# Attention and two gated MLPs on one core: another warm-up, another cut of the first MLP, and a planner's numbers anew

## The chip, the core and the metric

The kernel runs on one core of a Trainium2 chip. Time is the device time of one execution in microseconds (us). A core has five engines with queues of their own: TensorE (PE in the profile; its weight loads are PEld), VectorE (DVE), ScalarE (ACT), GpSimd (POOL) and SyncE (SP), which here issues all the transfers. They run side by side and wait for each other by semaphores only.

## The reference

Three stages follow each other; each takes the output of the one before as a matrix of 2304 tokens by 512.

```python
# attention: 4 images, 8 heads, 576 positions, 64 wide
rel = pos[:, None] - pos[None, :]
mask_plain = (rel >= 0) & (rel < 32)                      # heads 0 to 3
mask_dil = (rel >= 0) & (rel < 128) & (rel % 4 == 0)      # heads 4 to 7
attn = softmax(where(mask, q @ k.T / 8, -1e9));  x = attn @ v
# first gated MLP: d_model 512, d_ff 1536
xn = x / sqrt(mean(x * x) + 1e-6) * rms_g
x = (silu(xn @ w_gate) * (xn @ w_val)) @ w_out
# second gated MLP, with other weights of the same sizes
out = (sigmoid(x @ w2_gate) * (x @ w2_val)) @ w2_out
```

All in float32, except that the weights come as 64-bit numbers: the kernel reads both 32-bit words of each and makes a float32 of them.

## The kernel before, in words

**Products in two halves.** TensorE multiplies in a rounded format (fp32r). Each operand is split into a high part (a rounded copy, "hi") and a low part (the rest, "lo"), and each product is three matmuls: hi by hi, hi by lo, lo by hi. The helper `split` (lines 572 to 579) makes hi on ScalarE or VectorE and lo on GpSimd or VectorE.

**Attention.** Two heads are taken together, so there are four pairs for each of four images: pairs 0 and 1 with the plain mask, 2 and 3 with the dilated one. A pair is done in three groups of 192 positions, 48 groups in all. A group is twelve score matmuls (line 932), the mask and row maximum on VectorE (944), the exponential on ScalarE (950), the division, three transposes on TensorE (977), a copy (982), and twelve matmuls with the values (990). The first image's keys and queries are loaded by `first_qk` in long rows and turned on TensorE (784); those of the others are loaded in short rows and turned on VectorE (905). When all groups that a chunk of tokens needs are done, `x_norm` normalises it (sums at 1053, spreading at 1109, scaling at 1121) and splits it.

**First MLP.** The 1536 columns of d_ff are 12 blocks of 128. `PARAMS["holds"]` says in how many parts they are worked through and how many blocks each part keeps in the buffers: (4, 4, 4). In a part, all the chunks of tokens pass; their widths are `PARAMS["sizes"]`: four of 288 tokens and three of 384. For a chunk and a block, `mlp_step` makes the gate and value products (line 1278, twelve matmuls each) and their combination, and `y_group` the output product (line 1320, four times three matmuls). A part after the first loads the normalised chunk and the partial sums again and adds to them (line 1348). The first part runs while the attention is still going on. The weight buffers are two rings: 26 tiles of gate and value weights (four to a block) and 6 of output weights (one to a block).

**Weights.** `words` loads 512 KB into one of three buffers, and converts with one ScalarE (line 553) and four VectorE instructions (556, 559, 562, 565). Weights of the first part are split at once (`weight_plain`); all others are converted early, stored, and loaded again when due (`weight_ahead`, `weight_late`).

**Second MLP.** Three parts of four blocks; the products are formed with seven block products instead of eight (`unit`, line 1540; `y_products`, line 1458), for one image after the other.

**What sets the order.** No queue is written by hand. Each operation is added with an engine (or a choice of engines with a penalty each), an estimated cost, and a due time; `Line.emit` then plays the program through with these costs and, for each engine, takes the operation that can start first, and among those that can start at the same time the one with the earliest due time. The order found is the order of the queues, and is fixed in the program. The transfers are operations of SP, with an estimated rate. The numbers in `PARAMS` set due times (`att0`, `span0`, `lo1`, `hi1` and so on for the groups of each chunk; `wdue`, `wslope` for the weights; `ld_a` to `ld_d` for the first loads), penalties (`w_lo`, `ts`, ...) and earliest starts (`rel1`, `rel2`). Where an order is said in words ("wst order"), operations start in the order of the program.

**Warm-up and fillers.** `warm_up` writes zeros (line 805) and multiplies them (line 812): `warm_n` matmuls in threes, and later `warm_c` runs of `warm_m`, each of which may start from a time on and is left out if it could not start until another. `filler` (line 741) multiplies zeros into a bank that is about to be used, as many times as fit into the wait that the planner sees; `fill_from` and `fill_share` set from which wait on and how many.

Of the kernel before, what the change touches and what calls it, by code (L numbers as in the profile page):

```python
# [8 lines left out]
F32 = mybir.dt.float32  # L9
# [12 lines left out]


PARAMS = {
    "late": 0, "fill_share": -1.645, "fill_max": 6, "gather": -3.359, "w0_hi": 0.17,
    "w0_lo": 1.905, "h0_hi": 0.438, "h0_lo": 1.239, "x0_hi": 1.34, "x0_lo": 11.623, "ahead": 2,
    "todo0": 56.796, "todo1": 25.362, "todo2": 159.576, "todo3": 11.023, "xb_zero": 1.288,
    "stay": 0.699, "phase": 1.6, "fill_from": -2.118, "fill_gap": 0.077, "margin": 2922.227,
    "wait": 1.059, "w_sq": 42.802, "w_hi": 0.161, "w_lo": 1.285, "x_hi": 1.845, "x_lo": 0.0,
    "h_hi": 1.711, "h_lo": 0.003, "qk": 1.905, "norm": 0.0, "pts": 18.659, "o": 0.0, "snap": 7.898,  # L30
    "h_ahead": 98.614, "h2_ahead": -0.542, "evac": 0.038, "holds": (4, 4, 4), "norm_act": 0.0,
    "slack": 0.0, "share_v": 0.6, "share_p": 0.33, "cold": 1.7, "low": 0, "high": 0, "recip": 0.3,
    "rel1": 9.513, "span1": 1.059, "rel2": -0.748, "span2": -34.805, "ys": 37.984, "ts": 4.608,
    "cross": 0.06, "same": 0.04, "dma_lat": 1.7, "dma_rate": 330000.0, "by_pe": 0,
# [3 lines left out]
    "ld_v": -216.171, "ld_c": -161.215, "ld_d": -125.254, "lead": -1.421, "xdue": 1.319,  # L38
    "wdue": 0.824, "wslope": 1.126, "wload": -1350.235, "wload_step": -0.494, "warm_n": 12,
    "warm_t": 1.362, "warm_dt": -2.155, "warm_c": 19, "warm_m": 5, "warm_late": 13.822,  # L40
    "warm_due": 37.022, "mask_cost": 0.18, "exp_cost": 0.36, "s_cost": 0.546, "o_cost": 0.41,
    "t_cost": 0.265, "pt_lead": 1.847, "x_lead": 29.885, "wy_due": 1.584, "y_from": 5.448,
    "y_step": 0.787, "xb_due": -0.013, "y_last": 1.205, "xb_last": 0.798, "lo6": 114.943,
    "hi6": 132.108, "sizes": (288, 288, 288, 288, 384, 384, 384),
}
STEP = 6.24

# [32 lines left out]
class Line:  # L80
# [11 lines left out]

    def __init__(self):
        self.ops, self.writer, self.readers = [], {}, {}
        self.now = self.bus = 0.0
        self.last, self.mate, self.longer = {}, {}, 0.0
        self.work, self.window, self.warm, self.quad = 0.0, 0, False, False

# [43 lines left out]
    def add(self, eng, cost, fn, reads=(), writes=(), tiles=(), due=0.0, lat=0.0,  # L142
            release=0.0, until=None, other=(), bus=0.0, cols=0, fill=None, quad=False):

        o = Op()
        o.ways = {eng: (cost, fn, 0.0)}
        for kind, eng, cost, fn in [other] if other and isinstance(other[0], str) else other:  # L150
            o.ways[eng] = cost, fn, PARAMS[kind]
        o.eng, o.tiles, o.due, o.lat = None, list(tiles), due, lat
        o.seq, o.succs, o.end, o.release = len(self.ops), [], None, release
        o.until, o.bus = until, bus
        o.cols, o.fill, o.fills, o.quad = cols, fill, 0, quad
        preds = set()
        for key in reads:
            if key not in self.writer:
                raise KeyError(key)
            preds.add(self.writer[key])  # L160
            self.readers.setdefault(key, []).append(o)
        ahead = set()
# [18 lines left out]
        self.ops.append(o)  # L181
        return o
# [152 lines left out]
def attention_then_two_gated_mlps(  # L335
# [15 lines left out]
    nc = tc.nc  # L351
# [3 lines left out]
    P = 128  # L355
# [7 lines left out]
    T = S // 2  # L363
# [53 lines left out]
    add = line.add  # L417
    rings = {}

    def new(pool, tag, shape, dt=F32, bufs=2):  # L420
        ring = rings.setdefault((pool, tag), Ring(
            bufs, None if pool in ("mid", "bp") else 0.0, tag))
        return Tile(ring, lambda: pools[pool].tile(shape, dt, tag=tag, name=tag, bufs=bufs), shape)
# [37 lines left out]

    def rows(n, size):

        return n * (16.0 + 0.033 * size) / 16e3 * PARAMS["dma_rate"]


    ident = fixed("sb", "ident", [P, P])
# [288 lines left out]
    def first_qk(b, hp, staging, due, turn_due, engines=("SP", "SP")):  # L756


        dil = hp >= HP // 2
        hk = (b, hp)  # L760
        TP = S // 8
        kt, qt = qk_tiles(hk, turn_due)
        raws = []
        for nm, src, (ring, bufs), eng in zip("kq", (k, q), staging, engines):
            raw = new("sb", ring, [TP, 8, 2, D], F32, bufs)

            def load(raw=raw, src=src):
                (nc.scalar if eng == "ACT" else nc.sync).dma_start(
                    out=raw.t, in_=src[b, 2 * hp:2 * hp + 2].rearrange(
                        "e (p n) d -> p n e d", n=8))  # L770

            dma(load, rows(2 * S, 4 * D), writes=[("raw", nm, hk)] + ["o order"] * (ring == "wo"),
                tiles=[raw], due=due, cost=0.6, eng=eng)
            raws.append(raw)
        for nm, t, off, raw in (("k", kt, 32, raws[0]), ("q", qt, 0, raws[1])):
            for a in range(2):
                turned[0] += 1
                bank = new("ps", ("g", "y3", "v")[turned[0] % 3] if dil else ("g", "y3")[a],
                           [P, 4, TP], F32, 1)

                def turn(raw=raw, a=a, bank=bank):
                    for r in range(4):

                        nc.tensor.transpose(
                            bank.t[:, r], raw.t[:, 4 * a + r].rearrange("p e d -> p (e d)"),
                            ident[0:TP, 0:TP])

                add("PE", 0.255, turn, reads=[("raw", nm, hk), "ident"], writes=[("tb", nm, hk, a)],
                    tiles=[raw, bank], due=turn_due, cols=4 * TP, fill=filler(bank))

                def put(copy, t=t, off=off, a=a, bank=bank):
                    tt = t.t[:, off:off + S]
                    dst = tt.rearrange("p (r q a) -> p a r q" if dil else "p (q a r) -> p a r q",
                                       r=4, a=2)[:, a]
                    copy(out=dst, in_=bank.t)

                add("ACT", 0.36, lambda put=put: put(nc.scalar.copy),
                    reads=[("tb", nm, hk, a), ("kpad", hk)],
                    writes=[(nm + "T", hk, a)], tiles=[bank, t], due=turn_due,
                    other=("qk", "DVE", 0.36, lambda put=put: put(nc.vector.tensor_copy)))  # L800
        heads[hk] = kt, qt

    def warm_up(n, times):

        add("PL", 0.3, lambda: nc.gpsimd.memset(zeros.bitcast(F32), 0.0), writes=["warm"], due=-90)

        def some(n, cost, due, release, until=None):
            bank = new("ps", "y3", [P, T], F32, 1)

            def run():  # L810
                for _ in range(n):
                    nc.tensor.matmul(out=bank.t, lhsT=zeros[:, 0:P], rhs=zeros, start=True, stop=True)

            add("PE", cost, run, reads=["warm"], tiles=[bank], due=due, release=release,
                until=until, cols=n * T)

        for _ in range(n // 3):
            some(3, 0.128 * 3, -90, 0.0)
        for t in times:
            some(PARAMS["warm_m"], 0.128 * PARAMS["warm_m"], PARAMS["warm_due"], t,  # L820
                 t + PARAMS["warm_late"])

    def first_v(due):

# [978 lines left out]
```

## Time and profile before

| | us |
|---|---|
| median of 3 timed runs | 1041.44 (1040.22 to 1044.84) |
| the profiled execution's own time | 1038.41 |
| its span, from the first to the last instruction | 1036.3 |

| engine | busy us | share of the span | instructions |
|---|---|---|---|
| PE | 988.2 | 95% | 7624 |
| PEld | 957.7 | 92% | 7624 |
| DVE | 737.5 | 71% | 1757 |
| ACT | 499.6 | 48% | 1393 |
| POOL | 401.3 | 39% | 572 |

Busy time is the time in which at least one instruction of the engine runs; a matmul counts from its start to its end, and as matmuls overlap, time from one start to the next is shorter than the duration. The shares are means over stretches with different limits. The granted TensorE clock was 0.995 of full speed over the span.

### The profile page before, as it was taken

What the parts mean: (1) busy time and instruction counts of PE and PEld (TensorE: products, weight loads), DVE (VectorE), ACT (ScalarE), POOL (GpSimd) and SP (SyncE); (2) the same over time, 40 slices, a digit from 0 to 9 for tenths busy, and PEclk for the clock granted to TensorE, in tenths of its full rate; (3) what the DMA queues carried; (4) which work ended last, traced back from release to release, by engine and by line L of the source; (5) the groups of instructions that cost most, each with busy time, mean ns of one, the idle gap of its engine ahead of it and who ended that gap; (6) DMA issues with size and microseconds to landing.
All of it is one profiled execution on the core that took longest, in us unless ns stands there. A gap on an engine that the chain in (4) does not pass through costs nothing.

```text
span 1036.3 us, 21382 instructions
## 1 busy us (share of the span) xinstructions
PE 988.2 (95%) x7624; PEld 957.7 (92%) x7624; DVE 737.5 (71%) x1757; ACT 499.6 (48%) x1393; POOL 401.3 (39%) x572
## 2 busy tenths in 40 slices
PE   7889999999999999999999999999999999999997
PEld 6778888989999999999999989998889999999996
DVE  4898877688777778852444586778785769786765
ACT  4978577764542333422222354566563355434432
POOL 3355553466841001340011562346571256533220
PEclk9999999999999999999999999999999999999999
DMA  8859877859899889865776752635163553267633
GB/s 197 174 130 192 211 176 182 213 176 342 319 348 316 324 308 329 303 231 205 247 267 222 245 177 110 229 150 189 58 241 141 193 226 133 99 203 234 167 74 80
DMA packets 207690, 216.62 MB, mean 209 GB/s; under 512 B 136609, under 2 KB 163809, under 8 KB 207585
## 3 DMA queue, kind: packets, MB, share of 16 engines
q1 hardware_dynamic: 207584, 215.27, 65.2%
q8 instruction: 60, 0.98, 0.4%
q14 instruction: 46, 0.37, 0.1%
HBM read 145.23 MB, written 69.99 MB: 208 GB/s over the span
## 4 chain that ended last, share of the span: by engine, by line
PE 73%; DVE 14%; ACT 5%; DMA 3%; issue 2%; POOL 2%; SPq 1%; DVEq 0%; POOLq 0%; ACTq 0%
PE y L1320 13%; PE v L1278 13%; PE g L1278 13%; PE y L1458 11%; PE att L1540 8%; PE v L1540 6%; PE g L1540 5%; DVE t L1157 2%; ACT pr L950 2%; DVE t L1556 2%; PE att L932 1%; DVE h L579 1%; PE att L990 1%; DVE S L652 1%; DVE t L1578 1%
## 5 line engine op out<-in xcount | busy, mean ns | idle before, releaser
L576 POOL TENSOR_TENSOR h<-t,h 128x288 fp32r<-128x288 f32 (+1 forms) x164 | 149.6, 918 | 413.4 <-ACT h L572 365.6
L572 ACT CAST h<-t 128x288 fp32r<-128x288 f32 (+1 forms) x251 | 110.5, 444 | 175.1 <-DVE t L1301 89.7
L1320 PE MATMUL y<-h,wo 128*128 128x288 f32 (+1 forms) x1008 | 169.6, 315 | 0.3 <-ACT pt L1340 0.2
L1278 PE MATMUL v<-xo,w 128*128 128x288 f32 (+1 forms) x1008 | 166.7, 313 | 0.0
L1278 PE MATMUL g<-xo,w 128*128 128x288 f32 (+1 forms) x1008 | 166.7, 313 | 0.0
L1458 PE MATMUL y<-h,wo 128*128 128x288 f32 x1008 | 158.9, 298 | 5.8 <-ACT h L572 1.9
L1320 PEld LDWEIGHTS y<-h,wo 128*128 128x128 f32 x1008 | 154.6, 188 | 1.8 <-ACT pt L1340 0.4
L1278 PEld LDWEIGHTS g<-xo,w 128*128 128x128 f32 x1008 | 155.2, 189 | 0.3 <-issue 0.2
L1278 PEld LDWEIGHTS v<-xo,w 128*128 128x128 f32 x1008 | 154.4, 188 | 0.7
L1458 PEld LDWEIGHTS y<-h,wo 128*128 128x128 f32 x1008 | 142.5, 190 | 8.9 <-ACT h L572 3.0
L1301 DVE TENSOR_TENSOR t<-t,v 128x288 f32<-128x288 f32 (+1 forms) x84 | 41.4, 493 | 80.5 <-PE v L1278 76.3
L1411 DVE SCALAR_TENSOR_TENSOR pt<-y,pt 128x288 f32<-128x288 f32 x136 | 61.2, 452 | 50.1 <-PE y L1458 49.6
L1292 ACT ACTIVATE t<-g 128x288 f32<-128x288 f32 (+1 forms) x56 | 25.0, 447 | 94.8 <-PE g L1278 94.8
L1556 DVE TENSOR_TENSOR t<-t,att 128x288 f32<-128x288 f32 x96 | 43.0, 447 | 30.2 <-PE att L1540 26.0
L579 DVE TENSOR_TENSOR h<-t,h 128x288 fp32r<-128x288 f32 (+1 forms) x88 | 49.8, 571 | 14.3 <-ACT h L572 12.2
L950 ACT ACTIVATE pr<-pr,nmx 128x96 f32<-128x96 f32 x144 | 52.2, 365 | 11.6 <-DVE nmx L944 11.5
L562 DVE SCALAR_TENSOR_TENSOR wz<-wst,wz 128x512 int32<-128x512 int32 x72 | 55.8, 778 | 1.4
L565 DVE SCALAR_TENSOR_TENSOR wz<-wst,wz 128x512 int32<-128x512 int32 x72 | 55.6, 773 | 1.1
L553 ACT ACTIVATE wz<-wst 128x512 f32<-128x512 f32 x72 | 47.5, 668 | 17.6 <-DMA wst<-in_moe_w_gate_dram 7.8
L1540 PE MATMUL att<-xo,w 128*128 128x288 f32 x336 | 53.9, 295 | 1.0 <-DVE t L1556 1.0
L1540 PE MATMUL att<-wst,w 128*128 128x288 f32 x336 | 54.1, 296 | 0.0
L1157 DVE TENSOR_TENSOR t<-t,t 128x288 f32<-128x288 f32 x82 | 52.6, 642 | 1.3 <-POOL h L576 0.7
(193 smaller groups left out, 1764.4 us busy)
## 6 DMA issues: line engine op xcount, KB each, us to landing
z<-wz SPq DMA_DIRECT2D x60, 256.0 KB, 4.4
xo<-xs SPq DMA_DIRECT2D x23, 576.0 KB, 6.4
wst<-in_moe_w_gate_dram SPq DMA_DIRECT2D x24, 512.0 KB, 5.9
wst<-in_moe_w_val_dram SPq DMA_DIRECT2D x24, 512.0 KB, 5.4
wst<-in_moe_w_out_dram SPq DMA_DIRECT2D x24, 512.0 KB, 5.2
xs<-xs SPq DMA_DIRECT2D x21, 576.0 KB, 5.8
wst<-xs SPq DMA_DIRECT2D x18, 576.0 KB, 6.7
xo<-x SPq DMA_DIRECT2D x16, 576.0 KB, 5.5
```

Of the source, the lines that this page charges most:

```text
L562: add("DVE", Shared(0.595), lambda: nc.vector.scalar_tensor_tensor(out=z.t, in0=top(), scalar=-0x40000000, in1=z.t, op0=ALU.bitwise_and, o ...
L572: add("ACT", act(n), lambda: nc.scalar.copy(out=hi(), in_=src()), reads=reads, writes=[key] + [order] * bool(order), tiles=tiles + [dst], ...
L576: add("PL", pool(n), lambda: nc.gpsimd.tensor_tensor(out=lo(), in0=src(), in1=hi().bitcast(F32), op=ALU.subtract), reads=reads, writes=[ke ...
L579: other=(kind + "_lo", "DVE", dves(n), lambda: nc.vector.tensor_tensor(out=lo(), in0=src(), in1=hi().bitcast(F32), op=ALU.subtract)))
L950: add("ACT", PARAMS["exp_cost"], lambda u=u: nc.scalar.activation(out=pr.t[:, u], in_=pr.t[:, u], func=ACTF.Exp, bias=nmx.t[:, u:u + 1], s ...
L1157: add("DVE", dves(n), lambda: nc.vector.tensor_tensor(out=dst(), in0=a(), in1=c(), op=ALU.subtract), reads=reads, writes=writes, tiles=til ...
L1278: nc.tensor.matmul(out=bank.t, lhsT=w[:, l, cols], rhs=x[:, r, j], start=kk == 0 and n == 0, stop=kk == KD - 1 and n == 2)
L1320: nc.tensor.matmul(out=yb.t, lhsT=w.t[:, l, s], rhs=h.t[:, r], start=n == 0 and j == 0, stop=n == HOLDS[p] - 1 and j == 2)
L1411: add("DVE", dve(T), lambda: nc.vector.scalar_tensor_tensor(out=t.t[:, e, h], in0=bank.t, scalar=0.5, in1=t.t[:, e, h], op0=ALU.mult, op1= ...
L1458: nc.tensor.matmul(out=bank.t, lhsT=w.t[:, u, a, n], rhs=hs[u].t[:, d], start=first and u == 0 and m == 0, stop=u == NF // 2 - 1 and m == ...
L1540: nc.tensor.matmul(out=bank.t, lhsT=l.t[:, a, cols], rhs=r.t[:, d, j], start=first and j == 0 and m == 0, stop=j == 1 and m == 2, skip_gro ...
L1556: add("DVE", dve(T), lambda: nc.vector.tensor_tensor(out=t.t, in0=t.t, in1=bank.t, op=ALU.add), reads=[(key, uk)], writes=[ck[name]], tile ...
```

## The change

The new zeros' write is due first of all. The warm-up is one operation of 36 matmuls, in one bank that the later runs share. In the planner, the transfers begin at 1.6 us, rows cost 17.5 + 0.0355 per byte in place of 16.0 + 0.033, and a first load of keys or queries takes 1.1 us of SP in place of 0.6. The first MLP is cut into six chunks of 384 tokens and two parts of six blocks. Nearly all numbers in `PARAMS` are others; those that the prediction speaks of stand here, with some more.

```diff
-    "late": 0, "fill_share": -1.645, "fill_max": 6, "gather": -3.359, "w0_hi": 0.17,
+    "late": 0, "fill_share": -0.727, "fill_max": 6, "gather": 0.48, "w0_hi": 18.322,
...
-    "stay": 0.699, "phase": 1.6, "fill_from": -2.118, "fill_gap": 0.077, "margin": 2922.227,
+    "stay": 0.079, "phase": 1.6, "fill_from": 18.077, "fill_gap": -1.297, "margin": 2367.916,
...
-    "h_ahead": 98.614, "h2_ahead": -0.542, "evac": 0.038, "holds": (4, 4, 4), "norm_act": 0.0,
+    "h_ahead": 6.245, "h2_ahead": 1.536, "evac": 4.911, "holds": (6, 6), "norm_act": 0.904,
...
-    "turn0": -125.532, "turn1": -118.934, "turn2": -32.107, "att0": -371.487, "span0": 277.415,
-    "lo1": -10.504, "hi1": 2.607, "lo2": -1.115, "hi2": 13.348, "lo3": 1.504, "hi3": 89.26,
-    "lo4": 41.946, "hi4": 67.51, "lo5": 57.885, "hi5": 113.642, "ld_a": -294.837, "ld_b": -450.833,
-    "ld_v": -216.171, "ld_c": -161.215, "ld_d": -125.254, "lead": -1.421, "xdue": 1.319,
-    "wdue": 0.824, "wslope": 1.126, "wload": -1350.235, "wload_step": -0.494, "warm_n": 12,
-    "warm_t": 1.362, "warm_dt": -2.155, "warm_c": 19, "warm_m": 5, "warm_late": 13.822,
+    "turn0": 4.444, "turn1": -321.528, "turn2": -13.602, "att0": -191.799, "span0": 189.778,
+    "lo1": 2.246, "hi1": 21.361, "lo2": 1.646, "hi2": 44.88, "lo3": 40.955, "hi3": 63.261,
+    "lo4": 76.278, "hi4": 113.005, "lo5": 138.438, "hi5": 87.307, "ld_a": -107.09,
+    "ld_b": -123.163, "ld_v": -63.575, "ld_c": -63.972, "ld_d": -16.401, "lead": 1.069,
+    "xdue": 12.604, "wdue": -1.765, "wslope": 2.786, "wload": -675.096, "wload_step": 8.573,
+    "warm_n": 36, "warm_t": 1.316, "warm_dt": 0.302, "warm_c": 19, "warm_m": 5, "warm_late": 2.625,
...
-    "hi6": 132.108, "sizes": (288, 288, 288, 288, 384, 384, 384),
+    "hi6": 56.455, "sizes": (384, 384, 384, 384, 384, 384),
...
-        self.now = self.bus = 0.0
+        self.now, self.bus = 0.0, 1.6
...
-        return n * (16.0 + 0.033 * size) / 16e3 * PARAMS["dma_rate"]
+        return n * (17.5 + 0.0355 * size) / 16e3 * PARAMS["dma_rate"]
...
-                tiles=[raw], due=due, cost=0.6, eng=eng)
+                tiles=[raw], due=due, cost=1.1, eng=eng)
...
-        add("PL", 0.3, lambda: nc.gpsimd.memset(zeros.bitcast(F32), 0.0), writes=["warm"], due=-90)
-
-        def some(n, cost, due, release, until=None):
-            bank = new("ps", "y3", [P, T], F32, 1)
+        add("PL", 0.3, lambda: nc.gpsimd.memset(zeros.bitcast(F32), 0.0), writes=["warm"], due=-600)
+
+        bank = new("ps", "y3", [P, T], F32, 1)
+
+        def some(n, due, release, until=None):
...
-            add("PE", cost, run, reads=["warm"], tiles=[bank], due=due, release=release,
+            add("PE", 0.128 * n, run, reads=["warm"], tiles=[bank], due=due, release=release,
                 until=until, cols=n * T)
 
-        for _ in range(n // 3):
-            some(3, 0.128 * 3, -90, 0.0)
+        some(n, -90, 0.0)
         for t in times:
-            some(PARAMS["warm_m"], 0.128 * PARAMS["warm_m"], PARAMS["warm_due"], t,
-                 t + PARAMS["warm_late"])
+            some(PARAMS["warm_m"], PARAMS["warm_due"], t, t + PARAMS["warm_late"])
```

## Rows read from the trace of the kernel before

**Rows 1.** Stretches: length, busy us of each engine (instructions), clock, DMA share, GB/s.

```profile
31.00:46.00 15.00, 11.89 (x185) 10.25 (x185) 11.72 (x49) 14.84 (x49) 5.61 (x9) 1.00 1.03 206
46.00:73.40 27.40, 24.21 (x282) 20.98 (x279) 24.76 (x110) 20.98 (x83) 13.09 (x32) 0.94 0.40 91
73.40:118.00 44.60, 40.42 (x431) 37.14 (x430) 36.50 (x121) 32.98 (x117) 23.97 (x43) 1.00 0.88 192
118.00:235.00 117.00, 112.02 (x1170) 104.12 (x1169) 93.77 (x347) 82.38 (x297) 59.85 (x118) 1.00 0.76 196
235.00:594.30 359.30, 358.25 (x2333) 357.95 (x2333) 227.39 (x411) 122.17 (x254) 104.49 (x120) 1.00 0.81 286
594.30:780.00 185.70, 172.79 (x1243) 167.24 (x1242) 142.65 (x255) 104.81 (x270) 97.22 (x107) 0.99 0.46 168
780.00:1036.30 256.30, 244.76 (x1796) 240.16 (x1794) 184.10 (x395) 105.56 (x271) 85.01 (x102) 0.99 0.48 153
```

**Rows 2.** The same view for line 932 alone, the score matmuls.

```profile
0.00:73.40 73.40, 12.03 (x216) 9.81 (x216) 0.98 0.73 161
73.40:118.00 44.60, 5.27 (x96) 4.22 (x96) 1.00 0.88 192
```

**Rows 3.** Chain of waits in order of time: start, us, what.

```profile
249.22 2.08 PE y L1320 x12
...
302.00 1.60 PE y L1320 x12
```

**Rows 4.** Groups by line, shape: count | busy us, mean ns | idle before.

```profile
L1278 PE MATMUL g<-xo,w 128*128 128x288 f32 x576 | 85.7, 297 | 0.0
...
L1278 PE MATMUL g<-xo,w 128*128 128x384 f32 x432 | 81.0, 335 | 0.0
```

**Rows 5.** The same view, VectorE: weight conversion and additions of partial sums.

```profile
L562 DVE SCALAR_TENSOR_TENSOR wz<-wst,wz 128x512 int32<-128x512 int32 x72 | 55.8, 778 | 1.4
L565 DVE SCALAR_TENSOR_TENSOR wz<-wst,wz 128x512 int32<-128x512 int32 x72 | 55.6, 773 | 1.1
...
L559 DVE TENSOR_SCALAR wz<-wz 128x512 int32<-128x512 int32 x72 | 37.5, 527 | 1.2
...
L556 DVE TENSOR_SCALAR wz<-wz 128x512 f32<-128x512 f32 x72 | 35.7, 500 | 21.9 <-ACT wz L553 21.0
...
L1348 DVE SCALAR_TENSOR_TENSOR pt<-y,pt 128x288 f32<-128x288 f32 x32 | 12.8, 451 | 0.0
...
L1348 DVE SCALAR_TENSOR_TENSOR pt<-y,pt 128x384 f32<-128x384 f32 x24 | 12.3, 553 | 0.8 <-PE y L1320 0.8
```

**Rows 6.** Stretches for line 565 alone, the last instruction of a conversion.

```profile
0.00:73.40 73.40, 4.99 (x7) 0.98 0.73 161
73.40:118.00 44.60, 4.62 (x6) 1.00 0.88 192
118.00:140.00 22.00, 2.69 (x4) 1.00 0.84 212
```

**Rows 7.** Timeline, first 45 us: start, us, engine, what, idle before it.

```profile
6.05 9.41 PE L812 MATMUL y<-zeros 128*128 128x288 f32 x27 [6.05 <-POOL zeros L805]
...
15.50 0.68 PE L784 MATMUL v<-ident,xo 72*128 72x72 f32 x4
```

**Rows 8.** Stretches up to 118 us for line 741 alone, the fillers: their sum.

```profile
sum 118.00, PE 16.60 PEld 13.83; mean PE 3.32 PEld 2.77
```

**Rows 9.** Timeline of TensorE from 40 to 75 us.

```profile
41.69 0.45 PE L784 MATMUL g<-ident,wo 72*128 72x72 f32 x4
...
56.37 4.19 PE L741 MATMUL y<-zeros 128*128 128x288 f32 x30
...
63.57 1.06 PE L1278 MATMUL g<-xo,w 128*128 128x288 f32 x6
...
71.12 1.81 PE L1278 MATMUL g<-xo,w 128*128 128x288 f32 x6
```

**Rows 10.** Waits of TensorE from 594.3 us on: total us, times, longest.

```profile
PE g L1540 <- DVE t L1556: 9.2, 8, 2.2
```

More of the change, by code (lines that the diff above doesn't have):

```diff
@@ L24 @@
 PARAMS = {
-    "late": 0, "fill_share": -1.645, "fill_max": 6, "gather": -3.359, "w0_hi": 0.17,
-    "w0_lo": 1.905, "h0_hi": 0.438, "h0_lo": 1.239, "x0_hi": 1.34, "x0_lo": 11.623, "ahead": 2,
-    "todo0": 56.796, "todo1": 25.362, "todo2": 159.576, "todo3": 11.023, "xb_zero": 1.288,
-    "stay": 0.699, "phase": 1.6, "fill_from": -2.118, "fill_gap": 0.077, "margin": 2922.227,
-    "wait": 1.059, "w_sq": 42.802, "w_hi": 0.161, "w_lo": 1.285, "x_hi": 1.845, "x_lo": 0.0,
-    "h_hi": 1.711, "h_lo": 0.003, "qk": 1.905, "norm": 0.0, "pts": 18.659, "o": 0.0, "snap": 7.898,
@@ L31 @@
-    "h_ahead": 98.614, "h2_ahead": -0.542, "evac": 0.038, "holds": (4, 4, 4), "norm_act": 0.0,
-    "slack": 0.0, "share_v": 0.6, "share_p": 0.33, "cold": 1.7, "low": 0, "high": 0, "recip": 0.3,
-    "rel1": 9.513, "span1": 1.059, "rel2": -0.748, "span2": -34.805, "ys": 37.984, "ts": 4.608,
-    "cross": 0.06, "same": 0.04, "dma_lat": 1.7, "dma_rate": 330000.0, "by_pe": 0,
[3 rows of a table removed]
-    "ld_v": -216.171, "ld_c": -161.215, "ld_d": -125.254, "lead": -1.421, "xdue": 1.319,
-    "wdue": 0.824, "wslope": 1.126, "wload": -1350.235, "wload_step": -0.494, "warm_n": 12,
@@ L40 @@
-    "warm_t": 1.362, "warm_dt": -2.155, "warm_c": 19, "warm_m": 5, "warm_late": 13.822,
-    "warm_due": 37.022, "mask_cost": 0.18, "exp_cost": 0.36, "s_cost": 0.546, "o_cost": 0.41,
-    "t_cost": 0.265, "pt_lead": 1.847, "x_lead": 29.885, "wy_due": 1.584, "y_from": 5.448,
-    "y_step": 0.787, "xb_due": -0.013, "y_last": 1.205, "xb_last": 0.798, "lo6": 114.943,
-    "hi6": 132.108, "sizes": (288, 288, 288, 288, 384, 384, 384),
+    "late": 0, "fill_share": -0.727, "fill_max": 6, "gather": 0.48, "w0_hi": 18.322,
@@ new lines @@
+    "w0_lo": 9.893, "h0_hi": 0.962, "h0_lo": 0.547, "x0_hi": 1.123, "x0_lo": 0.752, "ahead": 2,
+    "todo0": 1353.619, "todo1": 6.063, "todo2": 24.639, "todo3": 0.613, "xb_zero": 0.211,
+    "stay": 0.079, "phase": 1.6, "fill_from": 18.077, "fill_gap": -1.297, "margin": 2367.916,
+    "wait": 0.585, "w_sq": 11.505, "w_hi": 0.053, "w_lo": 2.389, "x_hi": 0.018, "x_lo": 0.021,
+    "h_hi": 9.803, "h_lo": 0.002, "qk": 6.776, "norm": 0.38, "pts": 8.075, "o": 0.0, "snap": 2.373,
+    "h_ahead": 6.245, "h2_ahead": 1.536, "evac": 4.911, "holds": (6, 6), "norm_act": 0.904,
@@ new lines @@
+    "slack": 0.0, "share_v": 0.6, "share_p": 0.33, "cold": 1.7, "low": 0, "high": 0.39,
+    "recip": 0.3, "rel1": 84.815, "span1": -1.884, "rel2": 10.263, "span2": 0.38, "ys": 0.0,
+    "ts": 0.246, "cross": 0.06, "same": 0.04, "dma_lat": 1.7, "dma_rate": 330000.0, "by_pe": 0,
[3 rows of a table added]
+    "ld_b": -123.163, "ld_v": -63.575, "ld_c": -63.972, "ld_d": -16.401, "lead": 1.069,
+    "xdue": 12.604, "wdue": -1.765, "wslope": 2.786, "wload": -675.096, "wload_step": 8.573,
+    "warm_n": 36, "warm_t": 1.316, "warm_dt": 0.302, "warm_c": 19, "warm_m": 5, "warm_late": 2.625,
@@ L45 @@
+    "warm_due": 7.242, "mask_cost": 0.18, "exp_cost": 0.36, "s_cost": 0.546, "o_cost": 0.41,
+    "t_cost": 0.265, "pt_lead": 8.857, "x_lead": 16.276, "wy_due": 0.304, "y_from": 5.373,
+    "y_step": 0.87, "xb_due": -0.264, "y_last": 1.124, "xb_last": 9.329, "lo6": 108.574,
+    "hi6": 56.455, "sizes": (384, 384, 384, 384, 384, 384),
 }
```

## The prediction

> **What bounds the kernel now.** I read the stretches first: the busy time of each engine in windows cut where the work changes [rows 1]. They show four regimes. Up to 73.4 us the attention of the first 18 groups runs (216 score matmuls, 12 to a group [rows 2]); ScalarE is full in the middle of it (14.84 of 15.00 us) and TensorE waits or multiplies zeros. From 73.4 to 235 us the first MLP's first part runs between the other 30 groups: TensorE is idle for 44.60 - 40.42 = 4.2 us up to 118 and for 117.00 - 112.02 = 5.0 us after. From 235 to 594.3 us nothing but MLP matmuls is left, and TensorE is busy for 358.25 of 359.30 us: here only TensorE's own time counts. The second MLP follows with 12.9 and 11.5 us of idle TensorE, the last few of them the end of the program. So TensorE is the bound from 73.4 us on; in the first 118 us VectorE and ScalarE press on it.
>
> Then I read what a matmul costs. The chain of waits has twelve of 384 columns in 2.08 us and twelve of 288 in 1.60 us [rows 3], end to end, so 173.3 and 133.3 ns. (The mean duration in the lines view is longer, as matmuls overlap; I take from it the counts alone: 576 and 432 in one of the three products [rows 4].)
>
> **The change, part by part.** Terms are in us against the profiled execution: span 1036.3, its time 1038.4, so 2.1 lie around the span. The timed median, 1041.4, is 3.0 above that execution; I add 3.0 at the end.
>
> *Six chunks of 384.* Three products x 576 = 1728 matmuls of 288 columns become 3 x 432 = 1296 of 384: 1728 x 133.3 ns = 230.4 against 1296 x 173.3 ns = 224.6. **-5.8**, all on the engine that is the bound [rows 3, 4].
>
> Here a rule speaks against the change. The Trainium skill (TensorE: Matmul & The Clock Gate, the formula for the isolated gap) puts a full-clock matmul at columns divided by 2.4 GHz plus 2.5 ns: 122.5 and 162.5 ns, and the term would be 211.7 - 210.6 = -1.1. The chain disagrees: 13.3 ns beyond the columns at either width [rows 3]. I go by the chain.
>
> *Two parts of six blocks instead of three of four.* One reload of partial sums goes: 56 additions at line 1348 (32 + 24) become 24, some 25.6 - 13.3 = 12 us of VectorE [rows 5], with one store and one load of all partial sums and one load of all inputs. They lay where TensorE was idle 1.05 us in 359 [rows 1]: 0. A chunk passes six blocks in the first part instead of four, half as much MLP again, so the remaining attention has more to lie beside. MLP1 took 230.4 + 224.6 = 455.0, 2 before 73.4; of the 520.9 us from there to 594.3, 453 are MLP, 10.2 idle, and 57.7 are 30 groups, 1.9 a group. Those 57.7 stay. Of the idle 9.2 before 235 I take half away, **-4.6** (at best -9.2).
>
> *What is due sooner.* The first chunk now needs 18 converted weights, not 12. A conversion is four VectorE instructions, 500 + 527 + 778 + 773 ns = 2.58 us [rows 5], so six are 15.5. In the trace 7 were done by 73.4 and 6 more by 118, while VectorE worked 36.5 of 44.6 us [rows 1, 6]. But that stretch also finished 8 groups (96 / 12 [rows 2]); the new second chunk needs the two left of the first image and eight of the second, 20 in all, and 18 are there at 73.4. Six groups can move out, and the first chunk's matmuls are as long as the two first chunks of now (6 x 6.24 = 37.4, against 8 x 4.8 = 38.4). I take 0; from below 0, from above the whole 15.5. The six loads, 512 KB each, also go into a stretch where the DMA engines are 0.88 busy.
>
> *Buffers at the seams.* The ring of 26 weight buffers now holds 24 for one part (16 before), the ring of 6 output weights all 6. A split of the next part's weights waits for the last chunk's matmuls of the same block; behind it on ScalarE and GpSimd stand the running block's own casts, for which TensorE waits. Each block frees its buffers one step, 6.24 us, after the one before, five steps ahead of use, so I take **+1** (0 to one step, 6.2).
>
> *The start.* The zeros are written first instead of after the masks (TensorE waited 6.05 us for them [rows 7]); the masks come later by that one write, and no score needs them before the first keys have landed. The 27 warm-up matmuls become one run of 36; the later ones, which may start only within their time limit, mostly fall out. All that lies before the first transposes of keys at 15.5 [rows 7]: 0. The fillers, 16.6 us of zero matmuls [rows 8], go; they filled waits, so nothing is saved. The clock is a cost: granted 0.94 from 46 to 73.4 [rows 1], half speed (1.2 of 2.4 GHz) in one piece at the end of it, where six matmuls took 1.81 us against 1.06 earlier [rows 9]. Without the run of 30 fillers at 56.4 I count such pieces twice or three times: **+1.7** (0 to 5).
>
> That fits a rule, which alone gives no more: the Trainium skill (TensorE: Matmul & The Clock Gate, What's actually happening) has the clock throttled unless recent activity released it. By it the piece filled by the 30 zero matmuls would be slow and the sum the same.
>
> The first chunk is 384 wide: some ten steps in its chain grow by about 0.1 us (451 to 553 ns for one VectorE operation [rows 5]): **+1**. The order of loads and operations follows a planner whose small-row loads cost 9% more and whose issues on SP take 1.1 us, not 0.6; weights still come first, the first plain heads' keys and queries (two issues) now pass ahead of the 13 loads of values. The last head pair's keys reached TensorE at 41.7, and the first MLP matmul came 22 us later [rows 9]: a better order of ScalarE's queue is worth something there, **-3** (-10 to +7, the time between matmuls at 63.6 and 71.1 being 7.5).
>
> *The second MLP.* Only due times and preferences between engines move; there are 24.4 us of idle to win from [rows 1]. One late VectorE product alone costs 9.2 [rows 10]. I take **-1** (-12.9 to +12.9, the first stretch's idle once gone, once doubled).
>
> Sum: -5.8 - 4.6 + 1 + 1.7 + 1 - 3 - 1 = -10.7. The profiled execution would be 1027.7, the median 1031.
>
> **Rivals.** *Weights late in the first chunk (slower).* Conversions keep the present pace: 7 + 6 + 4 = 17 by 140 us [rows 6], the 18th at 142. TensorE would come to block six after 31.2 us of matmuls and some seven groups, 73.4 + 31.2 + 13 = 118: 24 late, of which four more groups (8) can fill. 16 are lost, 1047, and with the half of the idle not won (4.6) 1052. It decides the sign once more than 10 of these 24 us stay unfilled. For it: VectorE and DMA near full. Against: 5 of the conversions counted up to 140 were for later parts.
>
> *Given back (same).* The 5.8 is real, but seams, clock and second MLP stand at the upper ends of the small terms (5 + 3 over mine), or the idle stays: about 1039. For it: every re-ordered stretch has new waits. Against: nothing was idle at the present seams [rows 1].
>
> *A shorter start (faster still).* The order gains its 10, the 9.2 goes wholly, some of the second MLP's idle too: 1017. For it: 63 us before the first MLP matmul, 16.6 of zeros. Against: ScalarE full from 31 to 46.
>
> **How the numbers follow.** 0.5% is 5.2 us, about what a measurement of this kernel tells from no change: faster is below 1036.2, slower above 1046.6. Forecast 0.50 (1022 to 1040; 0.42 of it faster, 0.08 same); late weights 0.16 (slower 0.14, same 0.02); given back 0.16 (same 0.13, slower 0.03); shorter start 0.18 (faster). Faster 0.60, same 0.23, slower 0.17. The range leaves about 0.1 out at either end: 1012 to 1047.
>
> **What would show it.** Right: 2592 matmuls of 384 columns in lines 1278 and 1320, twelve in 2.08; the last of the first MLP near 584 instead of 594.3; no idle TensorE at the one seam between parts near 350 to 360. Start: the first full MLP product before 73.4. Wrong: TensorE waiting for w or wz between 75 and 125; idle in steps of 6 us at a seam; more half-clock pieces before 75 than three; a second MLP longer than 442 us.

## The result, and the profile after the change

The changed kernel took 1025.14 us in the median (1024.38 to 1027.10, 4 runs) against 1040.83 (4 runs) beside it on the same chip: a ratio of 0.9847 [0.9815, 0.9879], 15.7 us less. The forecast was 1031 (10.4 below the 1041.4 that it started from) and its range 1012 to 1047. The profiled execution took 1024.38 with a span of 1022.6, against 1038.4 and 1036.3: 13.7 less in the span. The last matmul of the first MLP ends at 585.05 instead of 594.34 (-9.3), and what follows takes 437.6 instead of 442.0 (-4.4).

First the stretches of the changed kernel, as in [rows 1]: length, busy time (instructions) of TensorE, its weight load, VectorE, ScalarE and GpSimd, granted clock, DMA share, GB/s. The cut at 594.3 became 582, 3 us before the first MLP ends, and that at 780 became 768.

```profile
15.00:31.00 16.00, 14.19 (x160) 11.98 (x158) 11.06 (x62) 14.43 (x55) 9.08 (x20) 0.71 1.02 219
31.00:46.00 15.00, 14.63 (x155) 12.15 (x152) 10.42 (x53) 12.47 (x50) 7.63 (x15) 0.54 0.94 210
46.00:73.40 27.40, 24.87 (x245) 21.32 (x245) 22.97 (x95) 21.88 (x81) 17.21 (x37) 0.81 0.49 114
73.40:118.00 44.60, 39.97 (x377) 34.83 (x375) 39.81 (x113) 30.01 (x102) 29.66 (x51) 0.96 0.91 190
118.00:235.00 117.00, 114.72 (x984) 106.16 (x985) 93.95 (x294) 72.50 (x246) 62.98 (x120) 0.99 0.76 196
235.00:582.00 347.00, 346.73 (x2077) 344.20 (x2076) 215.61 (x397) 119.82 (x245) 108.27 (x128) 1.00 0.67 228
582.00:768.00 186.00, 174.95 (x1260) 168.61 (x1259) 147.86 (x266) 97.30 (x259) 106.05 (x116) 1.00 0.47 171
768.00:1022.60 254.60, 243.58 (x1796) 238.35 (x1794) 182.63 (x393) 102.32 (x266) 91.48 (x109) 1.00 0.48 155
```

Read the fifth line first: idle TensorE is 117.00 - 114.72 = 2.3 us where it was 5.0, while the fourth stretch keeps 4.6 (4.2 before). Then the sixth: 0.3 us of idle in 347, with the one seam between parts inside. Then the clock of the first three: 0.71, 0.54 and 0.81, though TensorE is busy 14.63 of 15.00 us in the second. Before it was 1.00, 1.00 and 0.94 there.

The chain's unit, TensorE's timeline across the seam (start, us, engine, line, operation, count); the gate product at 358.15 is the first of the second part:

```profile
353.99 2.24 PE L1277 MATMUL v<-xo,w 128*128 128x384 f32 x12
356.07 2.24 PE L1319 MATMUL y<-h,wo 128*128 128x384 f32 x12
358.15 2.24 PE L1277 MATMUL g<-xo,w 128*128 128x384 f32 x12
360.23 2.24 PE L1277 MATMUL v<-xo,w 128*128 128x384 f32 x12
```

From start to start a run of twelve is 2.08 us, 173.3 ns each, as the 384-column chunks had in [rows 3]. All 2592 matmuls of the first MLP now have that width, 864 in each of the three products; two of the groups (count | busy us, mean ns | idle before):

```profile
L1319 PE MATMUL y<-h,wo 128*128 128x384 f32 x864 | 167.5, 338 | 0.3 <-DVE ms L1068 0.3
L1277 PE MATMUL g<-xo,w 128*128 128x384 f32 x864 | 164.9, 339 | 0.0
```

The first chunk, one gate product for each of its six blocks and the first of the next chunk (the first in two runs, with the value product behind it), with the two waits of TensorE over 1 us among them (in brackets: idle, and what ended it):

```profile
63.98 2.42 PE L1277 MATMUL g<-xo,w 128*128 128x384 f32 x9
...
67.80 0.80 PE L1277 MATMUL g<-xo,w 128*128 128x384 f32 x3
68.44 2.25 PE L1277 MATMUL v<-xo,w 128*128 128x384 f32 x12
...
70.77 2.33 PE L1277 MATMUL g<-xo,w 128*128 128x384 f32 x12
...
77.10 2.24 PE L1277 MATMUL g<-xo,w 128*128 128x384 f32 x12
...
86.54 2.35 PE L1277 MATMUL g<-xo,w 128*128 128x384 f32 x12
...
100.71 2.36 PE L1277 MATMUL g<-xo,w 128*128 128x384 f32 x12
...
112.75 0.68 PE L989 MATMUL att<-pts,v 96*64 96x64 f32 x12 [2.05 <-DVE ms L1068]
...
119.03 0.52 PE L1108 MATMUL att<-ident,rb 128*128 128x128 f32 x3 [2.41 <-DVE nmx L943]
119.30 3.69 PE L1277 MATMUL g<-xo,w 128*128 128x384 f32 x12
...
129.47 2.35 PE L1277 MATMUL g<-xo,w 128*128 128x384 f32 x12
```

A block's matmuls are 6.24 us long, so only the first blocks follow at their own pace; the fifth and sixth come 14.2 and 18.6 us after the one before, with attention groups between. A block needs three conversions (gate, value, output). Block five follows its own closely: the gate weights' conversion, the thirteenth, ends at 97.5, and the split into halves comes next. Block six does not: its gate weights, the sixteenth, are converted by 114.6, but GpSimd makes their low halves only behind the second chunk's normalisation:

```profile
113.09 0.56 POOL L1086 TENSOR_TENSOR rsa<-rsy 128x3 f32<-128x3 f32 x1 [0.84 <-DVE rsy L1072]
...
118.08 1.41 POOL L576 TENSOR_TENSOR w<-wz,w 128x256 fp32r<-128x256 f32 x2
```

The wait of 2.41 us before line 1108 is for the same normalisation: 1108 reads `rb`, which VectorE writes at line 1093 from 118.16 to 118.71; the line 943 that the view names runs behind it. The conversions are counted by their last instruction (stretches for line 565 alone, as [rows 6]; there 7, 6 and 4):

```profile
0.00:73.40 73.40, 7.64 (x9) 0.77 0.77 173
73.40:118.00 44.60, 6.85 (x8) 0.96 0.91 190
118.00:140.00 22.00, 2.00 (x2) 0.92 0.70 200
```

Seventeen were done by 118 where thirteen were, and VectorE was busy 39.81 of 44.60 us there, not 36.50.

### The profile page after: what moved, and what is told of

Same layout as the page of the kernel before. It is cut to its first block, busy times and chain, and to the rows that moved or that the text cites. A ratio compares the mean times of both kernels' runs of the same rounds, so it can differ in the third digit from the quotient of the medians.

```text
span 1022.6 us, 20013 instructions
## 1 busy us (share of the span) xinstructions
PE 983.6 (96%) x7096; PEld 947.1 (93%) x7096; DVE 733.8 (72%) x1686; ACT 476.9 (47%) x1308; POOL 441.9 (43%) x625
## 5 line engine op out<-in xcount | busy, mean ns | idle before, releaser
L576 POOL TENSOR_TENSOR h<-t,h 128x288 fp32r<-128x288 f32 (+1 forms) x144 | 136.7, 955 | 314.9 <-ACT h L572 248.1
L1319 PE MATMUL y<-h,wo 128*128 128x384 f32 x864 | 167.5, 338 | 0.3 <-DVE ms L1068 0.3
L1277 PE MATMUL g<-xo,w 128*128 128x384 f32 x864 | 164.9, 339 | 0.0
L1277 PE MATMUL v<-xo,w 128*128 128x384 f32 x864 | 163.0, 336 | 0.0
L1319 PEld LDWEIGHTS y<-h,wo 128*128 128x128 f32 x864 | 149.2, 188 | 2.1 <-issue 0.5
L1457 PEld LDWEIGHTS y<-h,wo 128*128 128x128 f32 x1008 | 141.3, 188 | 4.5 <-ACT h L572 2.3
L1300 DVE TENSOR_TENSOR t<-t,v 128x384 f32<-128x384 f32 x72 | 39.5, 549 | 70.5 <-PE v L1277 66.6
L579 DVE TENSOR_TENSOR h<-t,h 128x288 fp32r<-128x288 f32 (+1 forms) x96 | 62.1, 649 | 13.7 <-ACT h L572 11.3
L962 POOL TENSOR_SCALAR pr<-pr,rs 128x96 f32<-128x96 f32 x114 | 48.8, 441 | 45.6 <-DVE rs L957 30.5
L576 POOL TENSOR_TENSOR w<-wz,w 128x256 fp32r<-128x256 f32 x60 | 47.9, 812 | 23.1 <-ACT w L572 13.2
L576 POOL TENSOR_TENSOR w<-S,w 128x256 fp32r<-128x256 f32 x48 | 39.1, 824 | 37.9 <-DVE w L574 31.5
```

Source lines behind the costliest of these rows:

```text
L576: add("PL", pool(n), lambda: nc.gpsimd.tensor_tensor(out=lo(), in0=src(), in1=hi().bitcast(F32), op=ALU.subtract), reads=reads, writes=[ke ...
L579: other=(kind + "_lo", "DVE", dves(n), lambda: nc.vector.tensor_tensor(out=lo(), in0=src(), in1=hi().bitcast(F32), op=ALU.subtract)))
L1277: nc.tensor.matmul(out=bank.t, lhsT=w[:, l, cols], rhs=x[:, r, j], start=kk == 0 and n == 0, stop=kk == KD - 1 and n == 2)
L1319: nc.tensor.matmul(out=yb.t, lhsT=w.t[:, l, s], rhs=h.t[:, r], start=n == 0 and j == 0, stop=n == HOLDS[p] - 1 and j == 2)
L1457: nc.tensor.matmul(out=bank.t, lhsT=w.t[:, u, a, n], rhs=hs[u].t[:, d], start=first and u == 0 and m == 0, stop=u == NF // 2 - 1 and m == ...
```

## The experiments

Every kernel here is ordered anew by the planner after its edit, so an edit can move more than it names; what did move is read from the trace each time. The width of the chunks alone was not tried. Unless said otherwise, an edit is made to the changed kernel. Behind each median stands in brackets its ratio to the kernel before, timed beside it, with a 95% interval; the changed kernel's own is 0.9847 [0.9815, 0.9879].

**The parts, each way.** `e2_three_parts` and, on the kernel before, `e4_before_two_parts`:

```diff
-"holds": (6, 6)      # e2
+"holds": (4, 4, 4)
-"holds": (4, 4, 4)   # e4, before
+"holds": (6, 6)
```

> The changed kernel with three parts of four blocks (holds 4, 4, 4), chunks of 384 kept. Theory of the prediction: the two parts gave the 4.6 of idle under the attention less 1 at the seam, so without them 1028 to 1030 us, with more idle TensorE between 73 and 235. Rival: the parts gave nothing, because 18 weights instead of 12 in the first chunk take from VectorE what the longer MLP gives: 1023 to 1026.

> The kernel before with two parts of six blocks (holds 6, 6) and nothing else. Theory: the part of the gain that belongs to the parts alone, 3 to 4 us: 1036 to 1038 us. Rival (weights late in the first chunk): the old due times of weights and groups do not fit 18 weights, TensorE waits between 75 and 140 us for weights: 1045 to 1055.

Measured: 1064.96 us (1.0235 [1.0205, 1.0265]) and 1064.71 (1.0229 [1.0199, 1.0259]). Both lie far above what was expected. TensorE in e2, from block four of the first chunk on to the second chunk:

```profile
89.69 2.24 PE L1277 MATMUL g<-xo,w 128*128 128x384 f32 x12
...
130.40 0.92 PE L989 MATMUL att<-pts,v 96*64 96x64 f32 x12 [6.38 <-issue]
...
133.34 1.95 PE L1277 MATMUL g<-xo,w 128*128 128x384 f32 x5
```

Once the four blocks of the part are through (the output products end near 100), only attention is left for 33 us, in short runs with a wait before most of them. The order had put the second chunk behind it. In e4 the same happens at 181.1 to 206.1 and 232.5 to 256.9 (starts of two successive gate products each), later than the 75 to 140 of its rival. What follows: two parts alone are worth nothing, they cost 24 us with the old due times, as three parts cost 40 with the new ones. The term "idle under attention" belongs to the cut and the due times together and can't be split between them.

**When the weights are due.** `e10_weights_later` and `e9_weights_sooner`:

```diff
-"wdue": -1.765, "wslope": 2.786
+"wdue": -1.765, "wslope": 5.0     # e10
+"wdue": 0.824, "wslope": 1.126    # e9, the values of before
```

> The changed kernel with the weights of the first part due later (wslope 5.0: the 18th at 83 instead of 45.6). The prediction's slower rival made on purpose: if attention does not cover the wait, TensorE stands idle before the later blocks of the first chunk and the time is 1035 to 1050 us. Rival: the groups that move forward fill it, and they are then missing from later: 1024 to 1028.

> The changed kernel with the old due times of the first part's weights (wdue 0.824, wslope 1.126: the 18th due at 20 instead of 45.6), so that conversions go ahead of the second chunk's attention groups. Theory (the conversions set the pace of the first chunk, as the step of the sixth block starts at 119.3 us whether the first product is at 63.1 or 64.0): that step starts at 110 to 115, time 1020 to 1023 us. Rival (VectorE is full, what the weights win the groups lose, and the second chunk's norm is late instead): 1026 to 1032.

Measured: 1068.96 us (1.0282 [1.0256, 1.0309]) and 1037.32 (0.9983 [0.9963, 1.0002]). The gate products of blocks five and six in e10:

```profile
100.59 2.33 PE L1277 MATMUL g<-xo,w 128*128 128x384 f32 x12
...
140.52 2.48 PE L1277 MATMUL g<-xo,w 128*128 128x384 f32 x12
```

Up to block five it is the changed kernel; then block six comes 21 us later, its value and output weights converted at 129.9 and 134.9, and gaps of the same kind between two gate products follow at 153 to 191 and 223 to 261, with attention in short runs in them. The rival "weights late" exists, and block six needs to be only 21 us late, where the rival had 24, for 44 us in all instead of 16, as the gaps come again in the chunks after. In e9, blocks five and six and the second chunk:

```profile
108.48 3.58 PE L1277 MATMUL g<-xo,w 128*128 128x384 f32 x12
...
119.05 2.38 PE L1277 MATMUL g<-xo,w 128*128 128x384 f32 x12
...
141.79 3.55 PE L1277 MATMUL g<-xo,w 128*128 128x384 f32 x10
```

Eighteen conversions were through by 118, one more than in the changed kernel, yet block six stands where it did, and the second chunk starts 12 us later: the groups that VectorE set aside came after it, with one wait of 4.8 us for VectorE's scaling of the second chunk (L1120). The first MLP ends at 596.8. So sooner isn't better either; the theory that the conversions alone delay the first chunk fell. What happened is the rival's (what goes ahead on VectorE is missing elsewhere), and more of it: the time lies above the 1026 to 1032 that it gave.

**The planner's load times.** `e8_old_load_costs`:

```diff
-self.now, self.bus = 0.0, 1.6
+self.now, self.bus = 0.0, 0.0
-return n * (17.5 + 0.0355 * size) / 16e3 * PARAMS["dma_rate"]
+return n * (16.0 + 0.033 * size) / 16e3 * PARAMS["dma_rate"]
-tiles=[raw], due=due, cost=1.1, eng=eng)
+tiles=[raw], due=due, cost=0.6, eng=eng)
```

> The changed kernel planned with the old costs of the first loads (transfers from 0, rows 16.0 + 0.033 per byte, 0.6 us of issue); nearly the same order. Theory: the costs place operations that wait for loads behind those that do not, some stalls of 1 us each: 1026 to 1029 us. Rival: the order of the queues hardly changes, 1024 to 1026.

Measured: 1034.2 us (0.9926 [0.9894, 0.9958]), 9 more than the changed kernel. In the profile the first MLP ends at 592.3, 7.3 later, and the second is as long (437). The loads of the seventh and the tenth weight and the end of the seventh's conversion (rows of SP and of VectorE), first in the changed kernel:

```profile
39.55 0.43 SPq L532 DMA_DIRECT2D wst<-in_moe_w_gate_dram  x1
...
49.39 0.66 DVE L565 SCALAR_TENSOR_TENSOR wz<-wst,wz 128x512 int32<-128x512 int32 x1
...
50.12 0.39 SPq L532 DMA_DIRECT2D wst<-in_moe_w_gate_dram  x1
```

and in e8:

```profile
40.20 0.43 SPq L532 DMA_DIRECT2D wst<-in_moe_w_gate_dram  x1
...
52.39 13.56 SPq L843 DMA_DIRECT2D v<-in_v_dram  x22
...
64.07 0.66 DVE L565 SCALAR_TENSOR_TENSOR wz<-wst,wz 128x512 int32<-128x512 int32 x1
...
70.00 0.45 SPq L532 DMA_DIRECT2D wst<-in_moe_w_gate_dram  x1
```

A block of 22 small loads holds SP for 13.6 us (0.62 each). With the old costs the tenth weight's load stands behind it and leaves at 70.0, in the changed kernel ahead of it and leaves at 50.1. But the block is not where the delay begins. There are three load buffers, so the tenth load needs the one that the seventh conversion frees, and that conversion ends 15 us later in e8 (64.7, not 50.1), though its load left at the same time: VectorE begins it at 51.0 and ends it at 64.7, with the first chunk's normalisation and attention between. The eighth and ninth come 6 and 5 us later, with their loads on time too; once the buffer is free, the rest of the block and a few issues behind it cost the tenth load 5 us more. e8 reaches its first gate product sooner (59.17, not 63.98), and then falls back block by block, here the second and the sixth:

```profile
69.49 2.33 PE L1277 MATMUL g<-xo,w 128*128 128x384 f32 x12
...
125.79 3.22 PE L1277 MATMUL g<-xo,w 128*128 128x384 f32 x12
```

So the order made with the new load times matters, and not by an earlier start. The conversions from the seventh to the seventeenth come 3 to 15 us later in e8, at first because of VectorE's order and not of a late load; which of the moved operations costs the 7.3 us isn't shown.

**Clock and zero matmuls.** Old filler settings in the changed kernel (`e1_fillers`), the new ones in the kernel before (`e5_before_no_fillers`), fillers up to 62 us in every gap and, up to six at a time, in front of other matmuls (`e6_dense_fillers`), the same with e9's weights (`e12_dense_fillers_weights_sooner`), and the old warm-up (`e7_old_warm_up`):

```diff
-"fill_share": -0.727, "fill_from": 18.077, "fill_gap": -1.297   # e5: added to before
+"fill_share": -1.645, "fill_from": -2.118, "fill_gap": 0.077    # e1
+"fill_share": 0.6, "fill_from": 0.0, "fill_gap": 0.077          # e6, e12
-if o.eng == "PE" and o.fill and not swapped:
+if o.eng == "PE" and o.fill and start < 62.0:                   # e6, e12
-some(n, -90, 0.0)
+for _ in range(n // 3):                                         # e7, with warm_n 12, the
+    some(3, -90, 0.0)                                           # zeros due at -90 and the old times
```

> The changed kernel with the old filler settings (fill_share, fill_from, fill_gap); order and due times stay those of the changed kernel. Theory: the half-speed pieces (some 40 us of half clock between 14 and 123 us, 3.4 before) are there because the fillers are gone, and they cost time, since TensorE is busy for 28.8 of 31 us between 15 and 46: with fillers the clock stays full, the first MLP ends 3 to 6 us sooner, 1019 to 1022 us. Rival: ScalarE and the loads set the start, the slow matmuls lay in waits: clock up, time unchanged, 1024 to 1026. A second rival: the zeros themselves get in the way: over 1027.

> The kernel before with the filler settings of the changed one, so without fillers; its order of operations stays. Theory (the clock has a price): several half-speed pieces between 15 and 73 us where there was one, TensorE late in the chain of the first chunk, the first MLP ends 3 to 6 us later: 1044 to 1048 us. Rival (the fillers lay in waits and the clock is hidden too): 1039 to 1042.

> The changed kernel with zeros multiplied up to 62 us of the planner's time wherever TensorE's recent work is under 0.6 of full, up to six at a time (fill_share 0.6, fill_from 0, limited to start < 62). Theory: that holds the clock where the few fillers of the old settings did not; the first MLP starts 3 to 6 us sooner and the time is 1018 to 1022. Rival: the zeros stand in front of work that is ready and take as much as the clock gives: 1024 to 1030.

> e6 and e9 together: the clock held by dense fillers up to 62 us, and the weights due sooner. Theory (first chunk paced by weights, then by the start): the gains add, 1017 to 1021 us. Rival: no better than e9 alone, or worse by the zeros.

> The changed kernel with the old warm-up (zeros written after the masks, matmuls in threes and later fives, a bank each). Theory: the old warm-up stood in front of the first transposes (15.50 us before, 10.41 now, where the keys are waited for), so it puts them back to 15 and the first MLP product 2 to 5 us later: 1027 to 1030 us. Rival (the prediction's: nothing before 15.5 matters, the half clock eats the lead anyway): 1024 to 1026.

Measured: e1 1029.84 us (0.9875 [0.9828, 0.9921]); e5 1043.05 (1.0022 [0.9988, 1.0057]); e6 1027.44 (0.9865 [0.9808, 0.9923]); e12 1043.48 (1.0040 [1.0012, 1.0067]); e7 1025.80 (0.9845 [0.9795, 0.9895]). In e6 the stretches for the fillers' line, and the stretch from 31 to 46 us:

```profile
0.00:62.00 62.00, 27.84 (x132) 18.80 (x132) 1.00 0.86 179
```

```profile
31.00:46.00 15.00, 14.58 (x188) 12.34 (x188) 11.15 (x60) 12.42 (x47) 7.40 (x16) 1.00 1.18 205
```

27.8 us of zeros hold the clock at 1.00, where the changed kernel has 0.54 in the same stretch with TensorE as busy. And still block five comes at 100.6, block six at 119.4 and the end of the first MLP at 584.8 (changed kernel: 100.7, 119.3, 585.05). Up to block four e6 is 1.5 us ahead (85.04, not 86.54); block five's weights are converted at the same time as in the changed kernel (97.4 and 97.5), and the lead is gone. So what TensorE gains here at full clock ends in a wait for the other engines; how much of the full clock's gain the zeros themselves eat, e6 can't tell. The old fillers in e1 (9.6 us of zeros up to 118, 4.9 of them before 62) don't hold the clock at all, 0.52 from 31 to 46. In the kernel before, the lack of fillers (e5) also halves it:

```profile
31.00:46.00 15.00, 14.40 (x128) 12.75 (x126) 8.34 (x37) 12.42 (x37) 5.10 (x8) 0.50 0.98 196
46.00:73.40 27.40, 20.26 (x243) 16.72 (x244) 23.02 (x98) 20.76 (x82) 10.92 (x29) 0.75 0.36 86
```

There the first gate product comes at 67.2 instead of 63.6, but the first MLP ends only 1.4 later; the time can't be told from no change. e12 doesn't get e9's loss back, it is 6 us slower still; but its zeros put the first gate product at 67.5 (62.3 in e9), so it doesn't clear the clock either. e7 can't be told from the changed kernel: rewriting the warm-up is worth nothing that these runs can measure. The half clock isn't always free: in e7's profiled execution, at 1029.48, one piece goes from 31.8 to 55.7, the first gate product comes at 67.8 and the first MLP's end at 589.1; in e1's, at 1031.64, one goes from 31.5 to 58.8, with 69.1 and 592.2. The changed kernel, with 17 us at half between 31 and 52, has 63.98 and 585.05. As e7 and e1 carry other edits too, the clock isn't shown to be the cause.

**The second MLP.** The old due times of its operations (`e3_old_second_mlp`: thirteen values, among them `x_lead`, `wy_due`, `y_from`, `xb_due`, `pt_lead`, `ts`), and with these also the old preferences between engines (`e11_old_second_mlp_and_preferences`):

```diff
-"pt_lead": 8.857, "x_lead": 16.276, "wy_due": 0.304, "ts": 0.246, ...
+"pt_lead": 1.847, "x_lead": 29.885, "wy_due": 1.584, "ts": 4.608, ...   # e3, e11
-"w_hi": 0.053, "w_lo": 2.389, "h_hi": 9.803, "evac": 4.911, "ys": 0.0, ...
+"w_hi": 0.161, "w_lo": 1.285, "h_hi": 1.711, "evac": 0.038, "ys": 37.984, ...   # e11
```

> The changed kernel with the old numbers of the second MLP alone (snap, h2_ahead, x_hi, x_lo, ts, x_lead, wy_due, y_from, y_step, y_last, xb_due, xb_last, pt_lead). Theory: the 4.3 us that the second MLP became shorter (442.0 to 437.7) come from these numbers: 1028 to 1031 us, the part after the last matmul of the first MLP 441 to 444. Rival: they come from the state in which the first MLP leaves it (weights converted, buffers): unchanged, 1024 to 1026.

> As e3, and also the old numbers that act on both MLPs: evac, ys, w_hi, w_lo, h_hi, h_lo, and the due times and earliest starts of the second MLP's weights (todo0, todo1, rel2, span2). Theory (the second MLP's gain lies in its numbers): its length goes back from 437.7 to 441 to 443, time 1028 to 1031 us. Rival (it lies in the buffers and the cut of the first MLP): 437 to 440.

Measured: 1027.43 us (0.9882 [0.9841, 0.9922]) and 1032.77 (0.9927 [0.9904, 0.9950]). The second MLP takes 439.4 and 441.0 us in their profiles, and the first ends at 584.9 and 589.9. The stretches of it in e3:

```profile
582.00:768.00 186.00, 175.33 (x1244) 170.73 (x1244) 147.20 (x267) 100.46 (x259) 99.97 (x112) 0.97 0.45 166
768.00:1024.30 256.30, 244.85 (x1811) 240.51 (x1809) 185.64 (x400) 104.66 (x269) 86.75 (x104) 1.00 0.48 157
```

and in e11:

```profile
590.00:1030.90 440.90, 417.21 (x3035) 407.09 (x3034) 327.87 (x649) 209.97 (x541) 182.52 (x209) 0.99 0.47 159
```

Idle TensorE is 22.1 us in e3 and 23.7 in e11, against 22.1 in the changed kernel and 24.4 before [rows 1]. So e3 brings back no idle time, but 1.7 us of busy time, at a clock of 0.97 in the first stretch. That is not one execution's luck. In all five profiles with the old due times (before, e3, e4, e5, e11) two or three pieces at half clock lie in the middle of the second MLP; in the nine with the new ones (the changed kernel, e1, e2, e6 to e10, e12) there is none before the last 20 us of the program. The lengths don't overlap either: 436.4 to 439.1 us in those nine, 439.4 in e3, 441.0 to 443.0 in the other four. With e11, 3.5 of the 4.4 us are back, as its theory said: the second MLP's gain lies in these numbers. The 1.6 us of idle between e3 and e11 is a hint only, since the nine range from 20.1 to 23.1. Why the old due times go with half-clock pieces isn't shown. e11's first MLP ends 5 us later too, its first gate product 2.6 later (66.6); whether that is the order or the clock of this execution, as in e7, these runs don't tell.

## Why the prediction was right

The direction and the range held, the time came out 6 us below the forecast. Of the marks that it set, 2592 matmuls of 384 columns, the end of the first MLP (584 forecast, 585.05), the seam and the first full product (the value product at 68.44) came out as said; the half-clock pieces before 75 did not. Between the profiled executions, term by term:

| term | forecast | measured |
|---|---|---|
| widths | -5.8 | -5.8 by count and pitch, not tried alone |
| idle under attention | -4.6 | -3.0 (10.2 to 7.2 from 73.4 on; 9.2 to 6.9 up to 235) |
| seam | +1 | 0 |
| clock, wider first chunk, start and order | -0.3 | -0.5, the remainder to -9.3 |
| second MLP | -1 | -4.4 |
| sum | -10.7 | -13.7 |

*Widths.* The chain's 173.3 ns stood, as the row said. By the Trainium skill (TensorE: Matmul & The Clock Gate, Back-to-back issue gap) a run of twelve would take 1.95 us by the formula for an isolated gap; the trace has 2.08, and the measurement decides.

*Idle under attention.* Right in sign and two thirds of the size; the part before 118 won nothing: there the two waits above stand. The mechanism shows in where the attention went. Before, its last value product came at 225.1; now, with more MLP beside it, six groups' value products (72 matmuls of line 989) lie after 235, where TensorE is idle for 0.3 us:

```profile
235.00:290.00 55.00, 3.41 (x72) 2.58 (x72) 1.00 0.57 189
```

As a sum of its own the term is soft: in e6 the stretches from 73.4 to 235 have 6.6 and 2.4 us of idle, together as much as before, and the first MLP ends as early as in the changed kernel. The point that I missed is that the cut wins only with due times made for it (e2, e4).

*What is due sooner, 0.* Right for the sum, close to wrong in mechanism. The rival gave block six at 118 us and the 18th conversion at 142, and took that one for what block six waits for. Its gate product needs the 16th, which was there at 114.6; the 18th, at 131.8, holds the output weights, used at 134.7. Block six came at 119.3, and the gap of more than ten us before it was filled with groups but for 4.5 us. That is the rival's own condition (more than 10 of 24 unfilled) not met, and e10 shows the other side of it.

*The start and the order, -3.* Part of it came where it was forecast: the first gate product starts no sooner (63.98, was 63.57), but its two halves lie 3.8 us apart and not 7.5, and the value product behind it starts at 68.44, before at

```profile
73.11 1.97 PE L1278 MATMUL v<-xo,w 128*128 128x288 f32 x12
```

The lead is gone by block six. What is left of it can't be told apart in the -0.5 of four terms. The 9 us of e8 are no measure of it: like e2, e8 takes one edit out of a kernel whose other numbers were made with it. That "all before the first transposes at 15.5" is worth 0 fits the start of the first gate product, which didn't move. The 27 warm-up matmuls and their 6.05 us of waiting had kept TensorE until 15.5 [rows 7]; after the change it waits for the keys instead, and turns them at 10.41:

```profile
1.11 7.77 PE L813 MATMUL y<-zeros 128*128 128x288 f32 x36 [1.11 <-POOL zeros L805]
10.41 0.44 PE L784 MATMUL v<-ident,xo 72*128 72x72 f32 x4 [1.52 <-DMA xo<-in_k_dram]
```

e7 gives back only 1.6 of those five us (its first transposes come at 11.97), so what they are worth isn't shown by a run of its own.

*Clock, +1.7.* Too few pieces (three at most; it is half speed for some 34 us before 75, in four pieces), and the price too high for each: at the end of the first MLP the changed kernel is 0.3 us behind e6, and e5 1.4 behind the kernel before; 4 us, with a longer piece, go with it in e7's profiled execution. By the prediction's own mark, more than three pieces, this step was wrong.

*Second MLP, -1.* The term whose size was off most. Of -4.4, 2.4 is idle time and 2.0 is busy time, which the prediction did not think of: before, two half-clock pieces of 3.4 us lay in it (701 to 705, 882 to 886), now none but at the end of the program (e3, e11 and the other profiles above). The row on which the term stood, [rows 10], answers with (total us, times, longest):

```profile
PE g L1539 <- DVE t L1555: 6.7, 8, 1.5
```

The same eight waits, 2.5 us shorter.

So the sum's fit is in part luck: the second MLP gave 3.4 more than its term, 2.0 of it in clock that the prediction had not counted there, and hides that idle under attention gave 1.6 less.

The medians differ by 2.0 more than the spans. The profiled execution of the kernel before had nearly its highest clock (0.995), so its span is one of the short ones.

No version measured here beats the changed kernel: e7 is level with it, all others are slower or can't be told apart.

## What to carry to other kernels

Where a planner orders the work, price a re-cut together with its due times: either alone cost 24 to 40 us here, the whole change won 15.7. When a load leaves late, look first at what frees its buffer: in e8 a block of small loads (0.62 us of issue each) stood before it, but 15 of the 20 us of delay came from a conversion on VectorE. And before paying for a higher clock, find out which engine paces the stretch: here a start at half speed and one at full speed with zeros ended the first MLP within 0.3 us of each other (e6).

## What was not expected

The run time follows the mean granted clock from execution to execution of one kernel. Over the 44 runs of the kernel before beside the experiments it went from 1035.73 us at 0.995 to 1050.65 at 0.979, a fitted slope of about 0.75 us for each 0.001. 0.001 of the mean is 2.07 us at half speed, in which a full TensorE loses 1.04, so by this fit some 0.7 of the loss reached the end. Between the changed kernel and e6 that line doesn't hold: their profiles have 0.979 and 0.996, at 1022.6 and 1023.5 us of span; 34 of the changed kernel's 45 us at half clock lie before 66 us. Within e6 it does: 1023.47 and 1025.27 at 0.996, 1029.62 at 0.989, 1033.54 at 0.987. Why a piece falls where it does in one execution and not in the next stays open.

TensorE's clock can also be near half with the engine busy: 14.63 of 15.00 us at 0.54 with scores, transposes and attention products, against 14.58 at 1.00 when zero matmuls are among them (e6). The busy share misleads here, because at half speed the same work lasts longer. In e6 the zeros take half of that stretch (line 741 alone), so the rest, at full speed, is some 7 us of work:

```profile
31.00:46.00 15.00, 7.34 (x32) 4.51 (x31) 1.00 1.18 205
```
